# A fused top-k attention and ELU feed-forward kernel: ten steps instead of six in the step-by-step order, first scores head by head, and every second output tile in a bank of the first layer

## The chip, the cores and the metric

The kernel runs on one core of a Trainium2 chip. The metric is the device time of one execution in microseconds (us). The core's engines run side by side, each with its own queue of instructions in program order: TensorE (PE in the profile, with PEld for its weight loads), VectorE (DVE), ScalarE (ACT), GpSimd (POOL) and SyncE (SP), which here issues most DMAs.

## The reference

```python
q, k, v : (8, 8, 576, 64)            # batch, heads, tokens, head size, float32
scores = (q @ k^T) / sqrt(64)
kth    = 32nd largest score of each row
scores = where(scores >= kth, scores, -1e9)
attn   = softmax(scores)             # denominator + 1e-9
x      = (attn @ v)                  # to (8*576, 512)
h      = x @ w_in                    # (512, 2048)
g      = where(h > 0, h, exp(min(h, 0)) - 1)
out    = g @ w_out                   # (2048, 512) -> (4608, 512)
```

The two weight matrices arrive as float64, so the kernel reads them as pairs of 32-bit words and makes float32 of them itself.

## The kernel before, in words

**Attention steps.** The work is cut into 144 steps. A step (class `Step`) is 128 queries of one pair of heads, with all 576 keys: a score tile `sc` of 128 x 2 x 576. Four steps make a token tile of 128 queries over all eight heads (a remainder tile of 64 queries takes two steps), 36 token tiles' worth in all. For one step the engines do this:

- TensorE multiplies queries and keys (`scores`, into PSUM tiles `scps`); ScalarE copies the result to `sc` (L368).
- VectorE finds the 32 largest values of a row in four rounds of eight: `first_max` (MAX8, L373), then three calls of `next_max` (MATCH_REPLACE8, L379, and MAX8, L387). It is 14 passes over 128 x 576 values.
- GpSimd pushes all smaller scores far down. In the later order this is `mask`, three GpSimd passes a head (L399 to L401). In the order of the first steps it is `mask_early`: a small VectorE instruction (`field`, L413), small GpSimd ones (`minus`, `nth`, `pos`, `neg`), a ScalarE Relu (L428) and one GpSimd subtraction (L431).
- ScalarE takes the exponential with its row sums (`exp`, L439; at the end of a token tile it also adds the small constant to the sums, L445); TensorE transposes the result (`trans`, L481, L499) and multiplies by v (`attend`, L532, into `avps`).
- At the end of a token tile `sums` makes reciprocals of the row sums (VectorE, L451 and L452), sends them through DRAM to all partitions (SP, L456 and L468), ScalarE copies `avps` to `xT` (L542), and `normalise` multiplies them on GpSimd (L547).

**Feed-forward pieces.** Token tiles are grouped in 20 blocks of one to three tiles (the first seven blocks hold one tile each). When a block's tiles are normalised, `ffn_pieces` puts its work into a list: `hidden` pieces (first layer, L567, PSUM pool `ps_h` of two banks, tag "h"; then Exp, Relu, Relu on ScalarE, L581 to L583, and a subtraction on GpSimd, L584), then `project` pieces (second layer, L591, PSUM pool `ps_o` of one bank, tag "o"), eight pieces to a token tile; after the eighth ScalarE copies the bank to `osb` (L600) and SP writes it out. Each piece has a price in the code: 0.5 for a hidden piece of a one-tile block, 1.75 for a projection piece. `feed(n, part)` is called twice in a step; it spreads what is in the list over the steps to the next due time (`dues`), at most 6.6 a step in the first half of the run, and takes only pieces whose weights have been decoded.

**Weights.** There are 32 weight pieces. `split_weight` (ScalarE, L182 and L183) and, two slots later, `join_weight` (VectorE L188 and L189, GpSimd L193) decode one. `decode(n, place)` decides at which places of a step a slot is taken: four a step, five in steps 4 and 5. Slots end in step 7.

**The order of the work** is written out by hand in the loop over `n` at the end. For `n < EARLY` it is the early order, step by step: in step `n` the scores of step `n + 2` are computed, and step `n - 1` gets its `exp`, `trans`, `attend` and, if it ends a token tile, `sums` and `normalise`, all inside step `n`. `sums(last)` then stands inside the second `next_max` of the step. After that comes the order by pairs: in an even step the scores of steps `n + 2` and `n + 3`, and `attend` of steps `n - 4` and `n - 3`, so that a token tile is normalised two steps later than in the early order. `turns` says in which steps the queries and keys of a later pair of heads are transposed (L299, L307); `keep_kq` writes them to DRAM and `load_kq` brings them back for later token tiles (five buffers); `load_next` issues the next q and k loads on SP. `warm(n)` issues transposes of the identity on TensorE that nobody reads.

Of the kernel before, what the change touches and what calls it, by code (L numbers as in the profile page):

```python
# [10 lines left out]
FP32 = mybir.dt.float32  # L11
# [50 lines left out]
def kernel(  # L62
# [268 lines left out]
    def scores(u, half, copy=nc.scalar.copy):  # L331
# [35 lines left out]
                product(i, u.hps[0], i, slice(0, P), 0, ks)  # L367
        copy(u.sc[:, :, ks], ps[:, :, 0:HS])  # L368

    def first_max(u):  # L370
        u.m1 = small.tile([P, 2, 8], FP32, tag="m1", name="m1", bufs=2)
        for i in range(2):
            nc.vector.max(u.m1[:, i, :], u.sc[:, i, :])  # L373
        u.wk = wkpool.tile([P, 2, S], FP32, tag="wk", name="wk")
        u.m, u.cur = u.m1, u.sc
# [178 lines left out]
    def ffn_pieces(blk):  # L554
        N = blk.n * P


        G = {1: 4, 2: 2, 3: 1}[blk.n]

        def hidden(f, part):  # L560
            if part == 0 and f % NG == 0:
                blk.gT.append(gpool.tile([P, NG, T], FP32, tag="g", name="gT"))
            if part == 0 and f % G == 0:
                blk.h = ps_h.tile([P, WN], FP32, tag="h", name="hps")
            ps = blk.h[:, 0 : G * N].rearrange("p (f n) -> p f n", f=G)
            for i in range(part * NC // 2, (part + 1) * NC // 2):
                nc.tensor.matmul(  # L567
                    ps[:, f % G, :],
                    w_in[:, i, f * P : (f + 1) * P],
                    blk.xT[:, i, 0:N],  # L570
                    start=(i == 0),
                    stop=(i == NC - 1),
                )
            if part == 0 or f % G < G - 1:
                return

            f0 = (f - G + 1) % NG
            g = blk.gT[f // NG][:, f0 : f0 + G, 0:N]
            n = fpool.tile([P, WN], FP32, tag="n", name="n", bufs=2)
            n = n[:, 0 : G * N].rearrange("p (f n) -> p f n", f=G)  # L580
            nc.scalar.activation(n, ps, AF.Exp)  # L581
            nc.scalar.activation(g, ps, AF.Relu)
            nc.scalar.activation(n, n, AF.Relu, scale=-1.0, bias=1.0)  # L583
            nc.gpsimd.tensor_tensor(g, g, n, ALU.subtract)  # L584

        def project(s, part):
            if part == 0:
                blk.o = ps_o.tile([P, dm], FP32, tag="o", name="ops")
            step = NF // 8
            for f in range(part * step, (part + 1) * step):  # L590
                nc.tensor.matmul(  # L591
                    blk.o[:],
                    blk.gT[f // NG][:, f % NG, s * P : (s + 1) * P],
                    w_out[:, f, :],
                    start=(f == 0),
                    stop=(f == NF - 1),
                )
            if part == 7:
                o = fpool.tile([P, dm], FP32, tag="osb", name="osb", bufs=1)
                nc.scalar.copy(o[:], blk.o[:])  # L600
                for g in blk.tiles[s]:
                    p0 = g.cols.start - s * P
                    nc.sync.dma_start(out[g.rows, :], o[p0 : p0 + g.ql, :])

        t = max(0.25, 0.667 * blk.n / 3)
        return [
            (
                NC / 2 * t,
                lambda f=f, part=part: hidden(f, part),
                max(f // 4 * NC + NC - 1, 17 if f < NG else 19),  # L610
                blk,
            )
            for f in range(NF)
            for part in range(2)
        ] + [
            (1.75, lambda s=s, part=part: project(s, part), NF + (part + 1) * NF // 8 - 1, blk)
            for s in range(blk.n)
            for part in range(8)
        ]

    ffn = []
    owed = [0.0]

    def feed(n, part):
# [18 lines left out]
            owed[0] -= t  # L643


    EARLY = 6
    sizes = {0: (1, 1, 1, 1, 1, 1, 1, 2), 2: (2, 2, 2, 3), B - 2: (2, 2, 2, 2, 1)}
    steps, first, order = [], {}, []
    for b in range(B):
# [37 lines left out]

    def decode(n, place):

        if place in ((2, 3, 4, 5, 6) if n in (4, 5) else (3, 4, 5, 6)):  # L690
            weight_slot()

    todo, turns, blocks_at, behind = {}, {}, {}, {}
# [20 lines left out]
        elif p >= 2:  # L714
            at(p - 1, keep_kq, *pair)

    for u in steps[EARLY + 2 : EARLY + 4]:
        at(EARLY - 1, load_kq, u)
    for hp in range(1, NHP):
        at(hp, load_v, 0, hp)  # L720
    for b in range(1, B):
# [9 lines left out]
    with tc.manual_schedule():  # L731
        load_qk(0, 0)
        nc.scalar.activation(rec[:], rec[:], AF.Copy)
        for hp in (1, 2):
            load_qk(0, hp)
        load_weights(3)
        warm(16)
        for hp in range(2):
            transpose_qk(0, hp, shared=hp == 0)
            steps[hp].kq = {hp: kqT[0, hp]}  # L740
            scores(steps[hp], 0)
            scores(steps[hp], 1, nc.vector.tensor_copy if hp == 0 else nc.scalar.copy)
            if hp == 0:
                load_qk(0, 3)
        load_weights()
        load_v(0, 0)
        first_max(steps[0])
# [4 lines left out]
        for n in range(NS + 4):  # L752
            early = n < EARLY
            now, last, done = (
                steps[n + d] if 0 <= n + d < NS else None for d in (0, -1, -2)
            )
            for fn, args in todo.pop(n, []):
                fn(*args)
            gone = None
            if early:  # L760
                if n + 2 < NHP:
                    transpose_qk(0, n + 2)
                ahead = steps[n + 2]
                ahead.kq = {hp: kqT[0, hp] for hp in ahead.hps}
                for half in range(2):
                    scores(ahead, half)
                if n < EARLY - 1:
                    warm(24)
            elif n % 2 == 0:

                for d in (2, 3):
                    if n + d < NS:
                        for half in range(2):
                            scores(steps[n + d], half)
                    if d == 2:
                        for u in steps[n - 4 : n - 2]:
                            if not u.attended:
                                attend(u)
                                gone = u
                for u in steps[n + 4 : n + 6]:  # L780
                    load_kq(u)
                for fn, args in behind.pop(n, []):
                    fn(*args)
            if n in turns and not early:
                transpose_qk(*turns[n])
                load_next()
            if now and n > 0:
                first_max(now)
            if last and n > EARLY:
                biases(last, early)  # L790
                mask(last, 0)
            if early:
                decode(n, 0)
                feed(n, 0.5)
                if last:
                    exp(last, 0)
                    exp(last, 1)
                next_max(now, (n, 1))
                decode(n, 2)
                if last:  # L800
                    trans(last)
                feed(n, 0.5)
                next_max(now, (n, 3), last)
                decode(n, 4)
                if last:
                    attend(last)
                if n in turns:
                    transpose_qk(*turns[n])
                if n < EARLY - 1:
                    warm(24)  # L810
                next_max(now, (n, 5))
                tile_ends = last and last.ends
                mask_early(now, (lambda: normalise(last.g)) if tile_ends else None)
                decode(n, 6)
                if n >= NHP - 2:
                    load_next()
                continue
            decode(n, 0)
            feed(n, (0.3, 0.7)[n % 2])
            if now:  # L820
                next_max(now, (n, 1))
            decode(n, 2)
            if last:
                if n > EARLY:
                    mask(last, 1)
                exp(last, 0)
            if done and done.n in by_blocks:
                trans_blocks(done)
            elif done and not done.turned:
                trans(done)  # L830
            if now:
                next_max(now, (n, 3))
            decode(n, 4)
            if gone and gone.ends:
                normalise(gone.g)
            feed(n, (0.3, 0.7)[n % 2])
            if now:
                next_max(now, (n, 5))
            decode(n, 6)
            if last:  # L840
                exp(last, 1)
            if done and done.ends and not done.summed:
                sums(done)
            if n in blocks_at:
                transpose_blocks(*blocks_at[n])
# [35 lines left out]
```

## Time and profile before

| | |
|---|---|
| median of 3 runs | 1623.85 us (1623.75 to 1624.57) |
| profiled execution, its own time | 1623.01 us |
| its span in the trace | 1621.2 us |
| PE busy | 1560.3 us (96%) |
| DVE busy | 1474.9 us (91%) |
| POOL busy | 1141.6 us (70%) |
| ACT busy | 905.5 us (56%) |
| mean granted TensorE clock | 0.991 |

The profiled execution's own time is 1.8 us longer than its span. Busy times overlap, so they do not add up to the span. "Idle before" is the time in which an engine had nothing running before an instruction, and the releaser is the instruction whose end let it go on. For TensorE the profile counts two instructions for one float32 product in the code (a `trans` or `transpose_qk` transpose counts once).

### The profile page before, as it was taken

What the parts mean: (1) busy time and instruction counts of PE and PEld (TensorE: products, weight loads), DVE (VectorE), ACT (ScalarE), POOL (GpSimd) and SP (SyncE); (2) the same over time, 40 slices, a digit from 0 to 9 for tenths busy, and PEclk for the clock granted to TensorE, in tenths of its full rate; (3) what the DMA queues carried; (4) which work ended last, traced back from release to release, by engine and by line L of the source; (5) the groups of instructions that cost most, each with busy time, mean ns of one, the idle gap of its engine ahead of it and who ended that gap; (6) DMA issues with size and microseconds to landing.
All of it is one profiled execution on the core that took longest, in us unless ns stands there. A gap on an engine that the chain in (4) does not pass through costs nothing.

```text
span 1621.2 us, 28833 instructions
## 1 busy us (share of the span) xinstructions
PE 1560.3 (96%) x9948; PEld 1066.8 (66%) x9948; DVE 1474.9 (91%) x3070; ACT 905.5 (56%) x1857; POOL 1141.6 (70%) x1448
## 2 busy tenths in 40 slices
PE   7878999999999999999999999999999999999999
PEld 5765778777675858676565665565565585757665
DVE  7999999999999999999999999989999999899700
ACT  6875666555564756565574575465475364545321
POOL 3777777777786878778687687678677676767621
PEclk8989999999999999999999999999999999999999
DMA  9773454442121413232423524333332552453300
GB/s 311 246 219 120 147 180 141 131 129 104 42 111 51 152 58 117 72 94 82 119 71 104 183 80 116 108 102 103 109 113 76 151 161 96 121 135 89 87 13 14
DMA packets 226706, 188.70 MB, mean 116 GB/s; under 512 B 180480, under 2 KB 188672, under 8 KB 226560
## 3 DMA queue, kind: packets, MB, share of 16 engines
q1 hardware_dynamic: 224192, 186.26, 38.1%
q8 instruction: 79, 1.29, 0.3%
q10 hardware_dynamic: 2368, 0.59, 0.2%
q14 instruction: 67, 0.55, 0.1%
HBM read 151.26 MB, written 35.54 MB: 115 GB/s over the span
## 4 chain that ended last, share of the span: by engine, by line
PE 80%; DVE 8%; POOL 5%; ACT 3%; issue 2%; DMA 1%; SPq 0%; DVEq 0%; POOLq 0%; ACTq 0%
PE ops L591 27%; PE hps L567 27%; PE avps L532 9%; PE scps L348 9%; PE eps L481 6%; DVE m L387 3%; DVE wk L379 3%; POOL sc L401 1%; POOL gT L584 1%; POOL wk L399 1%; POOL wk L400 1%; PE eps L499 1%; DVE raw L189 1%; PE qkps L299 0%; DVE m L373 0%
## 5 line engine op out<-in xcount | busy, mean ns | idle before, releaser
L387 DVE MAX8 m<-wk 128x8 f32<-128x576 f32 x864 | 609.8, 748 | 0.0
L567 PE MATMUL hps<-xT,w_in 128*128 128x256 f32 (+2 forms) x2560 | 531.8, 363 | 13.5 <-POOL xT L547 9.1
L591 PE MATMUL ops<-w_out,gT 128*128 128x512 f32 x1152 | 518.8, 596 | 7.5 <-ACT osb L600 7.5
L567 PEld LDWEIGHTS hps<-xT,w_in 128*128 128x128 f32 x2560 | 406.5, 193 | 118.8 <-issue 19.7
L379 DVE MATCH_REPLACE8 wk<-m,wk 128x576 f32<-128x576 f32 x576 | 423.6, 743 | 0.0
L401 POOL TENSOR_TENSOR sc<-sc,wk 128x576 f32<-128x576 f32 x276 | 389.4, 1411 | 23.1
L591 PEld LDWEIGHTS ops<-w_out,gT 128*128 128x128 f32 x1152 | 210.1, 190 | 244.4 <-issue 219.1
L439 ACT ACTIVATE sc<-sc,neg 128x576 f32<-128x576 f32 x288 | 224.1, 779 | 215.0 <-POOL sc L401 210.6
L584 POOL TENSOR_TENSOR gT<-gT,n 128x512 f32<-128x512 f32 (+1 forms) x160 | 186.4, 1169 | 178.7 <-ACT n L583 175.9
L368 ACT COPY sc<-scps 128x576 f32<-128x576 f32 x287 | 169.3, 641 | 118.3 <-PE scps L348 115.4
L399 POOL TENSOR_SCALAR wk<-sc,nth 128x576 f32<-128x576 f32 x276 | 207.1, 750 | 26.9
L379 DVE MATCH_REPLACE8 wk<-m,sc 128x576 f32<-128x576 f32 x288 | 211.8, 744 | 0.0
L373 DVE MAX8 m<-sc 128x8 f32<-128x576 f32 x288 | 201.0, 740 | 0.1
L348 PE MATMUL scps<-kq 64*128 64x288 f32 (+3 forms) x1344 | 181.5, 419 | 20.2 <-ACT sc L368 10.9
L400 POOL TENSOR_SCALAR wk<-wk 128x576 f32<-128x576 f32 x276 | 184.3, 668 | 22.9
L532 PE MATMUL avps<-et,vE 128*64 128x128 f32 (+1 forms) x3200 | 176.7, 266 | 6.0 <-ACT et L486 3.6
L532 PEld LDWEIGHTS avps<-et,vE 128*64 128x64 f32 x3200 | 158.9, 137 | 31.9 <-issue 23.7
L486 ACT COPY et<-eps 128x1024 f32<-128x1024 f32 x132 | 132.7, 1005 | 68.9 <-PE eps L481 67.6
L581 ACT ACTIVATE n<-hps 128x512 f32<-128x512 f32 (+1 forms) x160 | 88.9, 556 | 134.8 <-PE hps L567 132.0
L348 PEld LDWEIGHTS scps<-kq 64*128 64x128 f32 (+1 forms) x1344 | 101.9, 175 | 88.7 <-issue 32.6
L481 PEld LDWEIGHTS eps<-ident,sc 128*128 128x128 f32 x1056 | 122.1, 141 | 49.2 <-issue 31.9
L481 PE MATMUL eps<-ident,sc 128*128 128x128 f32 x1056 | 138.1, 273 | 6.4 <-ACT sc L439 3.4
(74 smaller groups left out, 957.4 us busy)
## 6 DMA issues: line engine op xcount, KB each, us to landing
kq<-kqd SPq DMA_DIRECT2D x152, 576.0 KB
kqd<-kq SPq DMA_DIRECT2D x32, 576.0 KB
rb<-recd SPq DMA_DIRECT2D x64, 128.0 KB
out_dram<-osb SPq DMA_DIRECT2D x32, 256.0 KB
ed<-sc SPq DMA_DIRECT2D x12, 576.0 KB
et<-ed SPq DMA_DIRECT2D x48, 144.0 KB
kin<-in_k_dram SPq DMA_DIRECT2D x18, 256.0 KB
qin<-in_q_dram SPq DMA_DIRECT2D x17, 256.0 KB
```

The costliest lines, as they stand in the source:

```text
L348: nc.tensor.matmul(ps[rows, j, at : at + keys.stop - keys.start], u.kq[hp][r, 1, q0 : q0 + g.ql], u.kq[hp][r, 0, keys], start=True, stop=True,
L373: nc.vector.max(u.m1[:, i, :], u.sc[:, i, :])
L379: nc.vector.match_replace(u.wk[:, i, :], u.m[:, i, :], u.cur[:, i, :], TAKEN)
L387: nc.vector.max(u.m[:, i, :], u.cur[:, i, :])
L399: nc.gpsimd.tensor_scalar(pen, s, u.nth[:, i : i + 1], 2.0**100, ALU.add, ALU.mult)
L401: nc.gpsimd.tensor_tensor(s, s, pen, ALU.add)
L439: nc.scalar.activation(s, s, AF.Exp, bias=u.neg[:, i : i + 1], scale=scale, accum_out=g.den[:, at : at + 1],)
L481: nc.tensor.transpose(ps[:, i, c * P : (c + 1) * P], e[:, k0 + c * P : k0 + (c + 1) * P], ident[:],)
L532: nc.tensor.matmul(g.av[r, hp, 0:ql], vE[g.b, hp][:, i, (c + i) % (J + 1), :], u.et[:, at, q0 : q0 + ql], start=(c == 0), stop=(c == J),)
L567: nc.tensor.matmul(ps[:, f % G, :], w_in[:, i, f * P : (f + 1) * P], blk.xT[:, i, 0:N], start=(i == 0), stop=(i == NC - 1),)
L584: nc.gpsimd.tensor_tensor(g, g, n, ALU.subtract)
L591: nc.tensor.matmul(blk.o[:], blk.gT[f // NG][:, f % NG, s * P : (s + 1) * P], w_out[:, f, :], start=(f == 0), stop=(f == NF - 1),)
```

## The change

1. `EARLY` is 10 instead of 6. Steps 6 to 9 run in the early order. The `warm(24)` calls stay in steps 0 to 4, the transposed score tiles `et` of the first ten steps all go to the same spare buffer, and the keys and queries of steps 10 to 13 are loaded in steps 7 and 8 (before: at the start of steps 6 and 8).
2. `scores_by_head` computes the scores of step 0 head by head: each head's two halves of the keys, then one ScalarE copy of that head. Before, each half of the keys was computed for both heads, and the second copy was VectorE's. Nine idle transposes are put ahead of it.
3. The first weight load is issued before the loads of the third pair of heads, not after them.
4. `project` takes its PSUM bank from `ps_h` for every second token tile.
5. In steps 4 and 5 the fifth weight slot is at place 0 instead of place 2.

```diff
+    def scores_by_head(u):
+
+        u.sc = scpool.tile([P, 2, S], FP32, tag="sc", name="sc")
+        hp = u.hps[0]
+        for i in range(2):
+            ps = ps_x.tile([P, 2, JP], FP32, tag="x", name="scps")
+            r = slice(i * D, (i + 1) * D)
+            for half in range(2):
+                nc.tensor.matmul(
+                    ps[:, half, 0:HS],
+                    u.kq[hp][r, 1, u.g.qt * P : u.g.qt * P + u.g.ql],
+                    u.kq[hp][r, 0, half * HS : (half + 1) * HS],
+                    start=True,
+                    stop=True,
+                )
+            nc.scalar.copy(
+                u.sc[:, i, :].rearrange("p (n k) -> p n k", n=2), ps[:, :, 0:HS]
+            )
...
         def project(s, part):
             if part == 0:
-                blk.o = ps_o.tile([P, dm], FP32, tag="o", name="ops")
+
+                blk.o = (
+                    ps_h.tile([P, WN], FP32, tag="h", name="ops")
+                    if next(tile_count) % 2
+                    else ps_o.tile([P, dm], FP32, tag="o", name="ops")
+                )
...
+    tile_count = iter(range(B * S // P))
...
-    EARLY = 6
+    EARLY = 10
...
-        if place in ((2, 3, 4, 5, 6) if n in (4, 5) else (3, 4, 5, 6)):
+        if place in ((0, 3, 4, 5, 6) if n in (4, 5) else (3, 4, 5, 6)):
             weight_slot()
...
-    for u in steps[EARLY + 2 : EARLY + 4]:
-        at(EARLY - 1, load_kq, u)
+    for u, n in zip(steps[8 : EARLY + 4], (5, 5, 7, 7, 8, 8)):
+        at(n, load_kq, u)
...
         load_qk(0, 0)
         nc.scalar.activation(rec[:], rec[:], AF.Copy)
-        for hp in (1, 2):
-            load_qk(0, hp)
-        load_weights(3)
+        load_qk(0, 1)
+        load_weights(1)
+        load_qk(0, 2)
+        load_weights(2)
         warm(16)
         for hp in range(2):
             transpose_qk(0, hp, shared=hp == 0)
             steps[hp].kq = {hp: kqT[0, hp]}
-            scores(steps[hp], 0)
-            scores(steps[hp], 1, nc.vector.tensor_copy if hp == 0 else nc.scalar.copy)
             if hp == 0:
+                warm(9)
+                scores_by_head(steps[0])
                 load_qk(0, 3)
+            else:
+                for half in range(2):
+                    scores(steps[hp], half)
...
-                ahead.kq = {hp: kqT[0, hp] for hp in ahead.hps}
+                if ahead.n < 8:
+                    ahead.kq = {hp: kqT[0, hp] for hp in ahead.hps}
...
-                if n < EARLY - 1:
+                if n < 5:
                     warm(24)
...
-                if n >= NHP - 2:
+                if n == NHP - 2 or n in turns:
                     load_next()
```

More of the change, by code (lines that the diff above doesn't have):

```diff
@@ L808 @@
                     transpose_qk(*turns[n])
-                if n < EARLY - 1:
+                if n < 5:
                     warm(24)
```

## The prediction

> **What bounds the kernel now.** First the page's busy times and then the table of busy time by stage.
>
> ```profile
> PE 1560.3 (96%) x9948; PEld 1066.8 (66%) x9948; DVE 1474.9 (91%) x3070; ACT 905.5 (56%) x1857; POOL 1141.6 (70%) x1448
> ```
>
> ```profile
> 80.00:100.00 20.00, 14.54 (x125) 12.17 (x125) 19.97 (x36) 16.00 (x29) 14.65 (x16) 1.00 0.61 185
> 100.00:120.00 20.00, 14.65 (x105) 13.38 (x106) 19.96 (x40) 15.34 (x28) 14.68 (x19) 0.74 0.77 236
> 120.00:140.00 20.00, 16.59 (x92) 9.54 (x91) 20.00 (x39) 11.81 (x24) 16.77 (x19) 1.00 0.41 128
> 140.00:160.00 20.00, 16.07 (x107) 10.76 (x106) 19.97 (x43) 10.02 (x20) 13.76 (x18) 0.95 0.35 111
> 160.00:200.00 40.00, 39.87 (x331) 31.15 (x330) 36.79 (x80) 23.74 (x48) 30.07 (x39) 0.98 0.48 150
> 200.00:400.00 200.00, 199.75 (x1619) 151.99 (x1618) 195.08 (x413) 120.70 (x244) 148.46 (x190) 1.00 0.44 135
> 400.00:800.00 400.00, 391.54 (x2532) 274.83 (x2531) 396.88 (x838) 229.16 (x470) 306.42 (x393) 1.00 0.28 90
> 800.00:1200.00 400.00, 393.92 (x2265) 238.65 (x2264) 382.92 (x801) 229.21 (x499) 293.37 (x382) 1.00 0.38 111
> ```
>
> After the stage come its length, then PE, PEld, DVE, ACT, POOL, the clock, the DMA share and GB/s. Three regimes follow each other. To 160 us VectorE is full and TensorE is not: of 80 us it is idle 18. From 160 to 400 TensorE is full and VectorE waits 8 us. From 400 to 800 VectorE is full (99.2%), later TensorE (98.5%) more than VectorE (95.7%). TensorE's work can't shrink much, so a gain is TensorE time that is filled before 160 us, or a wait removed where it is full.
>
> The timeline of TensorE shows what it waits for in the early stage and at an output bank near the end; VectorE's shows the first wait of the second regime.
>
> ```profile
> 105.35 2.29 PE L348 MATMUL scps<-kq 64*128 64x288 f32 x8 [7.53 <-ACT sc L368]
> ...
> 158.02 7.25 PE L567 MATMUL hps<-xT,w_in 128*128 128x128 f32 x48 [2.84 <-POOL xT L547]
> ...
> 1575.38 14.00 PE L591 MATMUL ops<-w_out,gT 128*128 128x512 f32 x32 [0.68 <-ACT osb L600]
> ```
>
> ```profile
> 182.61 0.09 DVE L379 MATCH_VALUE_LOAD wk<-m,sc 128x8 f32 x1 [3.18 <-POOL sc L401]
> ```
>
> At 105 us step 6, the first in pairs, wants two steps' scores; the second stands behind a ScalarE copy that is itself queued behind the Relu of step 5. At 158 us the second token tile reaches the first layer: steps 4 to 7 were done, but the order by pairs normalises them only in step 10.
>
> **The longer early order (steps 6 to 9).** I followed `feed` through its own prices (near real times: a one-tile block's hidden pieces cost 16 and took 14.45 us, its projection 14 and 13.9). The second tile is now normalised in step 8 instead of 10, its due time is 9 instead of 10. Fed up to the end of step 13: before 53.0, after 58.25. The difference is three projection pieces of four, x 1.74 us = 5.2 us of TensorE work done ahead. By step 38, another due time, both stand at 210; so the 5.2 us come out of steps 14 to 37, where TensorE is full, and nothing of it is left for the tail.
>
> Does it fit? TensorE's rows: scores of a step 1.2, `trans` 1.14, `attend` 1.2, a turn 1.3. Step 8 has 7 of feed and 4.8 of these (11.8), step 9 has 10.6, against VectorE's 9.64 (a step without joins); so TensorE falls some 3 us behind there. Steps 10 to 13 need 23 to 25.75 of feed, 4.8 scores, three `trans`, one `attend`, two turns: 37, against 39.9 before and VectorE's 38.6 in four steps. TensorE enters step 14 about where it did, at 190 instead of 190.5, with 5.2 us less to do: **-5.7** at step 38.
>
> VectorE must follow. It loses or gains this:
> - `field` in four steps: the next instruction starts 0.08 later each, +0.3.
> - In steps 6 and 7 GpSimd has 2.8 us of subtraction a step for 5.7 of masks. VectorE's L189 takes 0.68, but 1.78 to 1.88 beside a GpSimd pass (114.59, 124.91): one of these goes at best a step, -0.7 (0 to -2.2).
> - The moved slot: L189 at place 2 of steps 4 and 5 took 1.78 and 1.79, beside a GpSimd join that had been queued behind the subtractions. At place 0 it comes 2.7 us after `field`, when the first subtraction has just begun (2.5), so it can be held there as well: -0.5 (0 to -2.2).
> - `sums` of the second tile moves into step 8. The sums come from ScalarE; step 4 shows the path:
>
> ```profile
> 66.66 0.17 DVE L413 TENSOR_SCALAR field<-m 128x2 uint32<-128x2 uint32 x1
> ...
> 76.29 0.19 DVE L451 RECIPROCAL rec<-den 128x8 f32<-128x8 f32 x1
> ```
>
> ```profile
> 68.24 1.63 ACT L428 ACTIVATE wk<-sc,pos,nth 128x576 f32<-128x576 f32 x2 [1.60 <-POOL pos L420]
> ...
> 73.64 0.21 ACT L445 ACTIVATE den<-den 128x8 f32<-128x8 f32 x1
> ```
>
> The sums are ready 7.2 us after `field`; 1.15 of that was a weight split, which step 8 lacks, so 6 to 7.2. VectorE in step 4 came 9.6 after `field`, with three joins between; in step 8 there are none and it comes after 0.1 + 1.33 + 1.31 + 1.33 + 1.31 = 5.4. It will wait, with MAX8 and all of step 8 queued behind: +1 (0.6 to 1.8; with a hidden group of ScalarE ahead 1.7 more).
> - Waits for `sc` L401: 3.18 in step 13 and 5.7 more in steps 14 to 38. They come from GpSimd queued behind first-layer pieces that TensorE had not finished. With one `attend` less ahead of these in step 12, I take 2 of the 3.18, and leave the 5.7 to give way as TensorE's load falls.
> VectorE's limit at step 38: 0.3 - 0.7 - 0.5 + 1 - 2 - 5.7 - 1 (start, below) = -8.6. TensorE's -5.7 is the smaller gain and decides.
>
> GpSimd in step 8 waits for the reciprocals' way through DRAM (7.5 us from 149.2 to 156.7): about 1.5 us with step 8's subtractions behind it, then `exp` and `trans` of step 8 on TensorE. That is the 3 us lag above. ScalarE gets a Relu pair of 1.63 a step, 6.5 in all, at 12 to 16 us of 20; hidden by its idle time, else it delays the score copies, needed two steps later. SP: the loads for steps 10 and 11 start a step later, behind `load_next`, which waits for a turn's transposes; the scores of step 10 are multiplied in step 8 and read in step 10, so a late load costs TensorE at most, 0 to 3. The q and k loads of the turns stay one to a turn, at the end of the step. The moved slot also puts a split (1.2) ahead of `exp` in steps 4 and 5: hidden by ScalarE's idle 1.9 to 2.7 before each Relu. `et` in one buffer: it is read before the next copy in TensorE's own order, 0.
>
> **The start.** The first MAX8 began at 11.15, after eight products (2.29), ScalarE's copy and VectorE's own copy. By head it needs four products and one copy of 0.64: 7.94 + 1.15 + 0.64 = 9.7, at full clock 9.2. The second head's copy ends 0.64 later, when MAX8 of the first (0.66) does: no wait.
>
> ```profile
> 6.00:8.00 2.00, 0.86 (x9) 0.99 1.37 226
> 8.00:10.00 2.00, 2.00 (x8) 0.50 1.37 201
> ```
>
> The clock fell to 0.50 after 1.1 us without products, and eight products took 2.29 instead of 1.24; nine transposes fill that gap: 0.11 each at full clock (24 took 2.60 at 24.04) or 0.21 (the first 16 took 3.32), from 6.8 to 7.8 or 8.7, so they delay the scores by 0 to 0.8. The Trainium skill, "TensorE: Matmul & The Clock Gate", Part 1, says that the clock halves only after a whole idle window of about 3.4 us, free-running, which this row contradicts unless the slow start counts as idle; by the rule the nine may change nothing, by the row they give 0.5 us, and the sum needs neither.
>
> But VectorE's next wait is for a split at 22.13 (0.69), behind the third pair's copies on ScalarE. That pair's loads now queue behind 1.5 MB of weights (5 us at 300 GB/s), the weights come earlier. From +1.5 to -1.9; I take -1, inside VectorE's limit.
>
> **The output bank.** The waits table has it:
>
> ```profile
> PE ops L591 <- ACT osb L600: 7.5, 11, 0.7
> ...
> PE hps L567 <- ACT gT L582: 4.4, 4, 1.6
> ```
>
> Eleven times TensorE waits 0.7 us for the copy of the tile before. With two banks in turn all go. 1.4 us lie where VectorE is the bound (400 to 800), 6.1 where TensorE is. Against it, `project` now can wait for a bank that the last but one hidden group has just filled; the second line says how often that distance already made TensorE wait, 4 times at 1.1 among some 280 groups. 18 tiles use such a bank: up to 1.4 us. **-4.7** (-7.5 to 0).
>
> **Sum.** 1623.0 (the profiled execution) - 5.7 - 4.7 = 1612.6; the median of before is 0.8 above that execution: 1613.
>
> **Rivals.**
> - *VectorE gets chained in steps 6 to 9* (slower). In each early step the Relu, the exponential and the transposes follow VectorE's last MAX8 through three engines in order. If VectorE must wait for what comes back, as TensorE did for 7.5 us in step 6, four waits of 4 us cost 16: 1623.8 + 16 - 4.7 (banks) - 1 (start) = 1634. It decides against the change from 10.4 / 4 = 2.6 us a step. For it: the early Relu already keeps ScalarE waiting 2.69 us at 102.04 with score copies queued behind. Against: from 40 to 100 us, in the same order and with more ScalarE work, VectorE was busy 59.87 of 60.
> - *Nothing comes of it*. VectorE keeps its pace to step 14, its waits for masks stay, and those for output banks return as waits for hidden groups: 1623.8 - 1 (start) - 1.4 (banks) + 1 (`den`) = 1622.4. For it: the planner evens out at step 38, and VectorE is full before 160 us.
> - *More*. VectorE's terms all at their good ends, 0.3 - 2.2 - 2.2 + 0.6 - 3.2 - 5.7 - 1.9 = -14.3, with TensorE following, and the banks' 7.5: 1602.
>
> **How the numbers follow.** Forecast 0.62 (1607 to 1619), more 0.10, nothing 0.13, chained 0.15. A measurement here can tell about 0.2% from no change. Faster 0.72, same 0.13, slower 0.15. The range 1604 to 1624 leaves out the chained case and a little at the lower end.
>
> **What would show it.** Right: TensorE's waits of 7.5 and 2.8 us gone, a first-layer piece of the second tile near 145 us, a VectorE wait of about 1 us for `den` in step 8, no wait on `osb`, step 38's first MAX8 (431.2 before) some 6 us earlier. Wrong: VectorE below 99% between 100 and 150 us, or TensorE idle as long as before up to 160 us, or new waits of `ops` on L582.

## The result

The changed kernel takes 1630.97 us (median of 6 runs, 1628.56 to 1632.9), the kernel before 1624.21 us (6 runs, 1623.75 to 1625.4). The ratio is 1.0039 with a 95% interval of 1.0026 to 1.0051: slower by about 6.3 us, where 10.8 us less was forecast, in a range from 1604 to 1624. The change is a sum of a gain and a larger loss. Run alone, the output banks are worth -10.4 us and the longer early order costs +14.8 us; the start cannot be told from nothing, and neither can the moved slot, which was run only together with the banks and the start.

### The profile page after: what moved, and what is told of

It reads as the page before. It is cut to its first block, busy times and chain, and to the rows that moved or that the text cites. A ratio compares the mean times of both kernels' runs of the same rounds, so it can differ in the third digit from the quotient of the medians.

```text
span 1627.2 us, 28888 instructions
## 1 busy us (share of the span) xinstructions
PE 1564.3 (96%) x9957; PEld 1072.5 (66%) x9957; DVE 1475.8 (91%) x3073; ACT 911.8 (56%) x1866; POOL 1133.0 (70%) x1444
## 4 chain that ended last, share of the span: by engine, by line
PE 66%; DVE 16%; POOL 6%; ACT 3%; DMA 3%; issue 3%; SPq 2%; DVEq 0%; POOLq 0%; ACTq 0%
PE hps L586 24%; PE ops L615 21%; PE avps L551 7%; PE scps L348 7%; DVE m L406 7%; DVE wk L398 7%; PE eps L500 5%; POOL sc L420 2%; POOL gT L603 1%; DVE m L392 1%; POOL wk L418 1%; POOL wk L419 1%; DMA vE<-in_v_dram 1%; PE qkps L299 1%; DMA ed<-sc 1%
## 5 line engine op out<-in xcount | busy, mean ns | idle before, releaser
L420 POOL TENSOR_TENSOR sc<-sc,wk 128x576 f32<-128x576 f32 x268 | 377.7, 1409 | 22.3
L458 ACT ACTIVATE sc<-sc,neg 128x576 f32<-128x576 f32 x288 | 223.9, 778 | 221.3 <-POOL sc L420 220.4
L418 POOL TENSOR_SCALAR wk<-sc,nth 128x576 f32<-128x576 f32 x268 | 199.6, 745 | 26.2
L419 POOL TENSOR_SCALAR wk<-wk 128x576 f32<-128x576 f32 x268 | 178.7, 667 | 22.1
L348 PE MATMUL scps<-kq 64*128 64x288 f32 (+1 forms) x1336 | 179.9, 418 | 11.8 <-ACT kq L294 6.7
L600 ACT ACTIVATE n<-hps 128x512 f32<-128x512 f32 (+1 forms) x160 | 88.7, 555 | 132.8 <-PE hps L586 127.9
```

The costliest lines, as they stand in the source:

```text
L348: nc.tensor.matmul(ps[rows, j, at : at + keys.stop - keys.start], u.kq[hp][r, 1, q0 : q0 + g.ql], u.kq[hp][r, 0, keys], start=True, stop=True,
L418: nc.gpsimd.tensor_scalar(pen, s, u.nth[:, i : i + 1], 2.0**100, ALU.add, ALU.mult)
L420: nc.gpsimd.tensor_tensor(s, s, pen, ALU.add)
L458: nc.scalar.activation(s, s, AF.Exp, bias=u.neg[:, i : i + 1], scale=scale, accum_out=g.den[:, at : at + 1],)
```

## The profile after

The profiled execution took 1628.94 us, with a span of 1627.2 us. The page's busy times:

```profile
PE 1564.3 (96%) x9957; PEld 1072.5 (66%) x9957; DVE 1475.8 (91%) x3073; ACT 911.8 (56%) x1866; POOL 1133.0 (70%) x1444
```

They hardly differ from before. The table by stage (stage, length, PE, PEld, DVE, ACT, POOL, clock, DMA share, GB/s) shows where the order went wrong:

```profile
100.00:120.00 20.00, 12.47 (x101) 11.28 (x99) 16.71 (x31) 12.81 (x25) 13.39 (x14) 0.83 0.39 112
120.00:140.00 20.00, 11.33 (x57) 7.01 (x58) 19.50 (x40) 11.40 (x22) 12.38 (x18) 0.74 0.23 81
140.00:160.00 20.00, 17.62 (x95) 10.42 (x94) 17.04 (x38) 11.31 (x23) 7.98 (x15) 1.00 0.61 190
160.00:200.00 40.00, 38.19 (x266) 28.92 (x265) 34.23 (x73) 24.84 (x48) 25.66 (x32) 0.96 0.57 170
200.00:400.00 200.00, 199.23 (x1631) 150.91 (x1630) 196.22 (x415) 122.21 (x249) 149.11 (x193) 1.00 0.43 134
```

TensorE was to be fuller between 100 and 200 us, by the 5.2 us of projections done ahead. It is emptier: 12.47 + 11.33 + 17.62 + 38.19 = 79.6 us, against 87.2 before (14.65 + 16.59 + 16.07 + 39.87). VectorE, which was full to 160 us, loses 3.3 us from 100 to 120 and 3.0 from 140 to 160.

TensorE's timeline shows the holes, with the releaser in brackets:

```profile
98.31 3.39 PE L586 MATMUL hps<-xT,w_in 128*128 128x128 f32 x28
108.33 1.97 PE L500 MATMUL eps<-ident,sc 128*128 128x128 f32 x8 [6.63 <-ACT sc L458]
...
127.83 1.97 PE L500 MATMUL eps<-ident,sc 128*128 128x128 f32 x8 [8.74 <-ACT sc L458]
...
142.66 1.04 PE L500 MATMUL eps<-ident,sc 128*128 128x128 f32 x8
...
158.28 2.40 PE L586 MATMUL hps<-xT,w_in 128*128 128x128 f32 x20
```

The waits of 7.53 and 2.84 us that the prediction wanted to remove are gone. In their place stand 6.63 us in step 6 and 8.74 us in step 7, ahead of the transposes of `trans(last)`. The eight transposes after each hole take 1.97 us, where they take 1.04 in step 8, at 142.66, in a stage with the clock at 1.00. The second token tile reaches the first layer at 158.28 us; before it was 158.02, and the forecast was near 145.

ScalarE's timeline shows why the transposes are so late, and VectorE's what that does to it:

```profile
102.22 1.62 ACT L447 ACTIVATE wk<-sc,pos,nth 128x576 f32<-128x576 f32 x2 [2.18 <-POOL pos L439]
103.75 0.65 ACT L182 ACTIVATE w_out<-w_out 128x512 f32<-128x512 f32 x1
104.31 0.65 ACT L183 ACTIVATE w_out<-w_out 128x512 uint32<-128x512 uint32 x1
104.86 1.15 ACT L368 COPY sc<-scps 128x576 f32<-128x576 f32 x2
105.91 0.60 ACT L600 ACTIVATE n<-hps 128x512 f32<-128x512 f32 x1
...
107.40 0.79 ACT L458 ACTIVATE sc<-sc,neg 128x576 f32<-128x576 f32 x1
...
112.95 0.60 ACT L600 ACTIVATE n<-hps 128x512 f32<-128x512 f32 x1 [1.44 <-PE hps L586]
...
114.44 0.68 ACT L182 ACTIVATE w_out<-raw 128x512 f32<-128x512 f32 x1
```

```profile
100.64 0.17 DVE L432 TENSOR_SCALAR field<-m 128x2 uint32<-128x2 uint32 x1
...
115.15 1.05 DVE L188 TENSOR_SCALAR w_out<-w_out 128x512 uint32<-128x512 uint32 x1 [3.21 <-ACT w_out L182]
...
142.86 0.20 DVE L470 RECIPROCAL rec<-den 128x8 f32<-128x8 f32 x1 [3.33 <-ACT den L464]
...
182.75 0.09 DVE L398 MATCH_VALUE_LOAD wk<-m,sc 128x8 f32 x1 [4.72 <-POOL sc L420]
```

The exponential of step 5 (L458, 107.40) stands on ScalarE behind the Relu, a weight split, two score copies and a hidden group (the Exp, Relu, Relu that follow a first-layer tile), while TensorE idles. Restarted at 108.33, TensorE delivers its next hidden group late, ScalarE's L600 waits 1.44 us for that, and behind it stands the weight split (L182, 114.44) that VectorE needs: VectorE waits 3.21 us. The same lag comes back in step 8 at `den` (3.33) and in step 12 at a mask (4.72; before, 3.18 in step 13).

The start of each step is the first MAX8 of it on VectorE. Against before, the changed kernel is 0.2 us late at step 6, 4.9 at step 7, 8.4 at step 9, 10.9 at step 14, 9.3 at step 38, 15.9 at step 90 and 7.8 at step 143. The prediction had 6 us early at step 38. (In the thirteen profiles with the old start, step 6 begins between 101.48 and 103.52 us, the kernel before being the earliest, so up to 2 us of such a difference can be the execution's.)

At the output banks the profile has no idle time left:

```profile
L615 PE MATMUL ops<-w_out,gT 128*128 128x512 f32 x1152 | 516.3, 597 | 0.0
```

## The experiments

Times are medians; the ratio is to runs of the kernel before on the same chip, with its 95% interval. For the parts alone the difference from before is taken from the ratio, later from the medians. "Profiled" spans have a run's noise in them: the same kernel's runs spread over up to 6 us.

### The parts alone

**Banks alone** (before, with the choice of `blk.o` from the change):

```diff
-                blk.o = ps_o.tile([P, dm], FP32, tag="o", name="ops")
+                blk.o = (
+                    ps_h.tile([P, WN], FP32, tag="h", name="ops")
+                    if next(tile_count) % 2
+                    else ps_o.tile([P, dm], FP32, tag="o", name="ops")
+                )
...
+    tile_count = iter(range(B * S // P))
```

> The kernel before with the bank alternation alone (part 4). If the longer early order is the whole loss, this is 3 to 6 us faster than before, with no wait of ops on osb (before: 7.5 us in 11 times). Rival: the banks tie the second layer to the first, the waits come back on gT and the time is the same within 1 us or some us slower.

1613.17 us, ratio 0.9936 (0.9924 to 0.9948): -10.4 us. The output layer's group before, then the same group with the banks and the one wait that was feared:

```profile
L591 PE MATMUL ops<-w_out,gT 128*128 128x512 f32 x1152 | 518.8, 596 | 7.5 <-ACT osb L600 7.5
...
L595 PE MATMUL ops<-w_out,gT 128*128 128x512 f32 x1152 | 515.9, 595 | 0.0
...
PE hps L567 <- ACT gT L582: 4.3, 4, 1.6
```

All eleven waits (7.5 us) went and no new ones came: 4.3 us on L582, as before (4.4). The profiled spans differ by 7.3 (1613.9 against 1621.2), which is the waits. Some of the gain lies between 400 and 800 us, the stage where the prediction had said that a TensorE wait costs nothing: VectorE is idle 1.7 us there instead of 3.1. The medians' further 3 us are not in this profile: its execution was the slowest of five (1615.72), the output layer's own time fell by 2.9 us and the first layer's grew by 4.0. The other pairs of kernels that differ in the banks alone agree that the banks are worth 8 to 11 us (below).

**The start alone** (scores by head, nine transposes, weights' loads):

```diff
-        for hp in (1, 2):
-            load_qk(0, hp)
-        load_weights(3)
+        load_qk(0, 1)
+        load_weights(1)
+        load_qk(0, 2)
+        load_weights(2)
...
+                warm(9)
+                scores_by_head(steps[0])
...
```

> The kernel before with the new start alone (parts 2 and 3: scores by head, nine idle transposes, weights loaded earlier). In the profile after, step 0 began 1.03 us earlier and step 1 only 0.24. Both theories: within 1 us of before. Rival for the loss: if the earlier weights push something else back, 2 us or more slower.

1624.36 us, ratio 1.0001 (0.9993 to 1.001): nothing.

**The early order alone**, with the loads and `load_next` that belong to it:

```diff
-    EARLY = 6
+    EARLY = 10
...
```

> The kernel before with EARLY = 10 alone (part 1 with what it needs: the loads of steps 10 to 13, the calls of load_next). Theory of the early order: step 14 begins about 11 us later than before (202.2 in the profile after against 191.3), VectorE waits about 3 us for a weight split in step 6 and 3 us for the sums in step 8, and the time is 8 to 14 us over before. Rival (the loss comes from the banks or from the moved slot): step 14 within 3 us of before and the time within 3 us.

1638.85 us, ratio 1.0091 (1.0078 to 1.0104): +14.8 us. Its TensorE has the same two holes and its VectorE the same three waits; a fourth comes at 651.56 us:

```profile
108.64 1.97 PE L481 MATMUL eps<-ident,sc 128*128 128x128 f32 x8 [6.97 <-ACT sc L439]
...
128.12 1.97 PE L481 MATMUL eps<-ident,sc 128*128 128x128 f32 x8 [8.75 <-ACT sc L439]
```

```profile
115.43 1.05 DVE L188 TENSOR_SCALAR w_out<-w_out 128x512 uint32<-128x512 uint32 x1 [3.17 <-ACT w_out L182]
...
651.56 0.09 DVE L379 MATCH_VALUE_LOAD wk<-m,sc 128x8 f32 x1 [3.41 <-POOL sc L401]
```

**Everything but the early order** (the change with `EARLY` back at 6, and with it the loads and `load_next`):

```diff
-    EARLY = 10
+    EARLY = 6
...
```

> The kernel after with EARLY back at 6 (parts 2 to 5 stay). Theory of the early order: no wait of VectorE in steps 6 and 8, step 14 within 1.5 us of 191.3, and 3 to 7 us faster than before. Rival: still slower than before by 2 us or more.

1613.98 us, ratio 0.9937 (0.9926 to 0.9949): start and slot add nothing to the banks. The parts sum to -10.4 + 14.8 + 0.2 = +4.6 against +6.3 (4.2 to 8.3) for the whole.

### Why the early order is slow far behind it

It is 9.6 us late at step 38 but 16.0 at step 84, although nothing of it lies there. `feed` carries a remainder, `owed`, from step to step. At the start of step 39 the list of pieces is the same in both kernels, but the remainder is -0.714 before and 0.047 with the longer early order. So later steps take other numbers of pieces: 20 steps from 40 to 74, and steps 117 and 118, get one more or one fewer.

**The early order with the old remainder** (the diff), and **the kernel before with the new one** (the same edit with 0.04687499999997202):

```diff
         for n in range(NS + 4):
+            if n == 39:
+                owed[0] = -0.7141666666666979
             early = n < EARLY
```

> e3_early10 (the longer early order alone) with the planner's carry (owed) at the start of step 39 set to the value that it has before the change, -0.714 instead of 0.047; from there on the pieces are the same, step for step, as before. Theory (the shifted pieces cost what is lost after step 38): step 38 begins 9 to 10 us late as in e3_early10 (9.6), step 143 no more than 11 late (15.3 in e3_early10), the time 4 to 6 us under e3_early10. Rival (a late start by itself makes more waits): step 143 still 14 to 16 us late.

> The kernel before with the planner's carry at step 39 set to the value of e3_early10 (0.047 instead of -0.714), and nothing else. Theory: nothing changes to step 38, and then 4 to 6 us are lost: 1628 to 1630. Rival: within 1.5 us of before.

1634.52 us (1.0065, 1.005 to 1.008), 4.3 less than without, and 1628.83 us (1.0029, 1.0018 to 1.004), 4.4 more than before. One remainder, exchanged both ways, is worth the same amount. It is lost on VectorE between 400 and 800 us: with the new remainder VectorE is idle 7.1 us there instead of 3.1 in the kernel before, and 6.4 instead of 2.5 with the early order. VectorE's timeline of the kernel before with the new remainder has the wait that the early order had at 651.56, while with the old remainder VectorE has no wait between 640 and 670 us:

```profile
643.56 0.09 DVE L379 MATCH_VALUE_LOAD wk<-m,sc 128x8 f32 x1 [3.41 <-POOL sc L401]
```

and its table row for that stage (stage, length, DVE, clock, DMA share, GB/s) is

```profile
400.00:800.00 400.00, 392.86 (x830) 1.00 0.27 88
```

The next experiments all keep the old remainder, so that only the steps up to 38 are in question: +10.5 us are left.

### Which wait in steps 6 to 13

**A weight slot of step 6 earlier**, so that VectorE's split is ahead of the late hidden group:

```diff
-        if place in ((2, 3, 4, 5, 6) if n in (4, 5) else (3, 4, 5, 6)):
+        places = (2, 3, 4, 5, 6) if n in (4, 5) else (3, 4, 5, 6)
+        if place in ((0, 4, 5, 6) if n == 6 else places):
```

> e5_carry with the first weight slot of step 6 at place 0 instead of 3, so that its split is ahead of the hidden pieces' activations on ScalarE. Theory (VectorE's 3.2 us in step 6 come from a split queued behind activations that wait for TensorE): no wait for w_out L182 in step 6, step 7 begins at most 2 us late (5.2 in e3_early10), and the time is 2 to 4 us under e5_carry. Rival (the wait only moves, because ScalarE and TensorE are late anyway): step 9 as late as before (8.6).

**The turns of steps 7 to 9 later**, so that a turn's copy is not ahead of the Relu and the exponentials that `den` needs:

```diff
-                if n in turns:
+                if n in turns and n < 6:
                     transpose_qk(*turns[n])
...
                 mask_early(now, (lambda: normalise(last.g)) if tile_ends else None)
+                if n in turns and n >= 6:
+                    transpose_qk(*turns[n])
```

> e5_carry with the turn's transposes of steps 7 to 9 behind mask_early instead of ahead of it. Theory (the sums of step 8 are late because the Relu of step 7 stands behind the copy of that turn on ScalarE): the Relu of step 7 no longer waits for TensorE, the wait for den in step 8 falls from 3.3 us to under 1.5, step 9 is about 2 us less late than in e3_early10 (8.6), and the time is 1 to 3 us under e5_carry. Rival: the wait for den stays over 2.5 us.

1633.70 us (1.0058, 1.0043 to 1.0073) and 1635.69 us (1.007, 1.0053 to 1.0087): -0.8 and +1.2, both within the error, where 2 to 4 and 1 to 3 us less were expected. VectorE's waits in the first (before the edit 3.08, 3.26 and 4.71):

```profile
118.35 1.04 DVE L188 TENSOR_SCALAR w_out<-w_out 128x512 uint32<-128x512 uint32 x1 [1.20 <-ACT w_out L182]
...
145.01 0.20 DVE L451 RECIPROCAL rec<-den 128x8 f32<-128x8 f32 x1 [4.36 <-ACT den L445]
```

and in the second:

```profile
143.25 0.20 DVE L451 RECIPROCAL rec<-den 128x8 f32<-128x8 f32 x1 [2.10 <-ACT den L445]
...
185.43 0.09 DVE L379 MATCH_VALUE_LOAD wk<-m,sc 128x8 f32 x1 [5.80 <-POOL sc L401]
```

Each edit shortened the wait that it aimed at, and the next wait grew by 1.1 us. So these waits look like symptoms of one lag.

**The step's whole feed ahead of the transposes** in steps 6 to 9, so that TensorE has work while the exponential is on its way:

```diff
-                feed(n, 0.5)
+                feed(n, 1.0 if n > 5 else 0.5)
...
-                feed(n, 0.5)
+                feed(n, 0.0 if n > 5 else 0.5)
```

> e5_carry with the whole feed of steps 6 to 9 ahead of the transposes of the step before, instead of half of it. Theory (in the early order TensorE stands still until the exponential of the step that VectorE has just finished, 6.6 and 8.8 us in steps 6 and 7, because only half a step's feed lies ahead of it): these two waits fall by 5 us or more together, the turn of step 7 is copied earlier, the wait for den in step 8 falls under 2 us, step 14 begins 7 to 9 us late instead of 12, the time 2 to 5 us under e5_carry (1634.5). Rival (the path from VectorE's last MAX8 over GpSimd and ScalarE sets the step, whatever TensorE does): step 14 within 1 us of e5_carry's.

1626.98 us, ratio 1.0018 (1.0008 to 1.0027): 7.5 us less than without it. TensorE's timeline:

```profile
107.77 1.16 PE L567 MATMUL hps<-xT,w_in 128*128 128x128 f32 x8 [3.21 <-ACT gT L582]
110.53 1.97 PE L481 MATMUL eps<-ident,sc 128*128 128x128 f32 x8 [1.60 <-ACT sc L439]
...
124.75 1.41 PE L481 MATMUL eps<-ident,sc 128*128 128x128 f32 x8 [0.87 <-ACT sc L439]
```

and VectorE's:

```profile
137.08 0.20 DVE L451 RECIPROCAL rec<-den 128x8 f32<-128x8 f32 x1 [0.67 <-ACT den L445]
...
177.16 0.09 DVE L379 MATCH_VALUE_LOAD wk<-m,sc 128x8 f32 x1 [4.74 <-POOL sc L401]
```

The hole of step 7 is down to 0.87 us, that of step 6 to 3.21 and 1.60, VectorE's 3.1 us wait of step 6 is gone and that for `den` is 0.67. So 7.5 of the 10.5 us come from TensorE having no work ahead of the transposes.

**All three edits together**:

> e5_carry with the three repairs together: feed ahead, the first slot of step 6 at place 0, the turns behind mask_early. Theory: no wait over 1.5 us on VectorE in steps 6 to 9, step 10 begins 1 to 4 us late instead of 9, the time 5 to 8 us under e5_carry: 1627 to 1630, still not under before, since the wait of step 12 for a mask stays. Rival (each repair moves the wait to the next engine): step 10 still over 6 us late.

1635.11 us, ratio 1.006 (1.0045 to 1.0075), where 1627 to 1630 was expected. The other two edits took back all that the feed had gained. TensorE's timeline:

```profile
110.74 2.08 PE L567 MATMUL hps<-xT,w_in 128*128 128x128 f32 x8 [6.05 <-ACT gT L582]
...
135.89 2.29 PE L348 MATMUL scps<-kq 64*128 64x288 f32 x8 [3.56 <-ACT kq L294]
```

With the fed pieces ahead TensorE depends on ScalarE's hidden group, and the earlier split now stands in front of that: it waits 1.75 us for GpSimd's join and puts the group (L581) off from 106.64 to 109.63; TensorE waits 6.05 us instead of 3.21. The later turn puts its copy (134.85) behind the Relu of step 7 (133.32), and step 10's scores wait 3.56 us for it. Edits that each moved about 1 us alone cost 8 us on top of the feed.

**No feed in step 10** (at both of its calls of `feed`), on top of the feed ahead, against the 4.74 us wait of step 12:

```diff
-            feed(n, (0.3, 0.7)[n % 2])
+            feed(n, 0.0 if n == 10 else (0.3, 0.7)[n % 2])
```

> e8_feed_first with no feed-forward pieces in step 10 (they follow in steps 11 to 38; from step 39 the pieces are those of before). Theory (the mask of step 10 waits on GpSimd behind a first-layer group that TensorE, 7 us behind VectorE at the change of order, delivers late): the wait of 4.7 us in step 12 falls under 2, step 14 begins 2 to 3 us late instead of 5, the time 1624 to 1626 (e8: 1627.0). Rival (the group then stands ahead of another mask, in step 11 or 12): the sum of VectorE's waits in steps 11 to 14 stays over 4 us and the time within 1 us of e8.

1627.01 us, ratio 1.0017 (1.0008 to 1.0026): nothing. VectorE's timeline:

```profile
174.09 0.09 DVE L379 MATCH_VALUE_LOAD wk<-m,sc 128x8 f32 x1 [1.18 <-POOL sc L401]
...
226.25 0.09 DVE L379 MATCH_VALUE_LOAD wk<-m,sc 128x8 f32 x1 [2.70 <-POOL sc L401]
```

The wait shrank by 3.6 us and 2.7 of it came back in a later step. At step 14 this kernel is only 1.9 us late, at step 18 again 4.7 and at step 38 6.0 (the feed ahead alone: 5.4).

The holes can also be read from TensorE's windows alone (stage, length, PE, clock, DMA share, GB/s), first the early order alone, then with the feed ahead (and the old remainder):

```profile
100.00:200.00 100.00, 79.25 (x514) 0.90 0.47 143
```

```profile
100.00:200.00 100.00, 86.19 (x568) 0.93 0.49 147
```

Before it was 87.2. Even the best early order, without its holes, leaves TensorE no fuller than the order by pairs.

### The banks with repaired early orders

The banks were added to the last three kernels: to all three edits, to the feed ahead, and to the feed ahead with no feed in step 10.

> e9_three with the bank alternation. If the parts add up, the time of e9_three less 10 (e1_banks took 10.4 off before). If the repaired early order is worth keeping it comes under 1613, the time of the banks alone; I expect 1616 to 1620.

> e8_feed_first with the bank alternation. If the parts add up: 1627.0 less 10.4, about 1616.6, over the banks alone (1613.2).

> e11_no_feed10 with the bank alternation: e11's time less 10.4, so 1614 to 1616 by the first theory, still no better than the banks alone (1613.2); by the rival about 1616.6.

1625.55 us (1.0005, 0.9995 to 1.0014), 1616.36 us (0.9952, 0.9937 to 0.9968) and 1618.62 us (0.9961, 0.9946 to 0.9976): 9.6, 10.6 and 8.4 us below the same kernels without the banks. None is better than the banks alone, 1613.17, the lowest time of this study; everything but the early order, 1613.98, cannot be told from it.

## Why the prediction was wrong

- **"Does it fit?" is the step that failed.** It summed TensorE's work per step and VectorE's time per step and set the larger against the other. It did so for steps 8 and 9 and for 10 to 13; steps 6 and 7, where the holes came, were not summed at all. But TensorE takes its work in order: in the early order only a step's scores and half a step's feed lie ahead of `trans(last)`, and that needs the exponential of a step which VectorE has only just finished. Nothing was summed for the way from VectorE's last MAX8 over GpSimd, ScalarE's Relu, splits, copies and hidden group to the exponential: `field` ends at 100.81 and the transposes start at 108.33, 7.5 us later. In the order by pairs the transposes of a step come a step later, behind more of other steps' work. Putting the feed into that time gave 7.5 of the 14.8 us back.
- **The -5.7 us at step 38 never came.** TensorE between 100 and 200 us was busy 79.6 us instead of 87.2, and with the holes repaired 86.2. The waits of 7.53 and 2.84 were removed as forecast, but in the repaired kernel TensorE is still idle 14.1 us between 100 and 240 us, against 13.1 before: for copies of transposed scores, hidden activations, exponentials and turn copies instead of mostly score copies.
- **"Nothing of it is left for the tail" was wrong by 4.3 us.** The list was the same at the end of step 38, as the prediction said; the planner's remainder was not, by 0.76 of a unit. The prediction followed `feed` through its prices and read off the pieces, not the remainder.
- **The wait for `den` in step 8** was forecast at +1 (0.6 to 1.8) and came to 3.33. The path was right and the size wrong: it took ScalarE to be on time, and the lag of steps 6 and 7 stood ahead of it. Without that lag it was 0.67, inside the forecast.
- **The L401 wait** was to lose 2 of 3.18 us; it became 4.72, a step earlier. Taking 3.6 us of it away changed nothing, so its size in the sum meant nothing either.
- **The start** was forecast at -1, out of a range from +1.5 to -1.9 that was not followed further. The first MAX8 came 1.03 us earlier than in the profile before, but by step 1 only 0.24 of that was left, and the start alone gave 0.2 us more, which is nothing. Much of the 1.03 belongs to that one profile: in the twelve others with the old start the first MAX8 begins at 10.18 to 11.03 us, with the new start at 10.12 to 10.64.
- **The clock.** The row on which the nine transposes rest was one execution's. The twelve other profiles with the old start have the same gap of 1.1 us ahead of the first scores, and in all of them the clock is 1.00 from 8 to 10 us and the eight products take 1.24 us, as in the banks alone:

```profile
8.49 1.24 PE L348 MATMUL scps<-kq 64*128 64x288 f32 x8 [1.14 <-DVE kq L292]
```

With the nine transposes the clock is 1.00 too, and the products take 1.37: as a rule there was nothing for them to win. The Trainium skill, "TensorE: Matmul & The Clock Gate", Part 1, makes the drop depend on a whole idle window of about 3.4 us. In the sixteen traces the granted clock does change only in steps of 3.41 us, which fall at another moment in each execution, but the stretch ahead of a drop is not always idle: in 110 drops TensorE was busy for 0 to 55% of it. The kernel before had the 55%, ahead of the drop at 7.96 us (stage, length, PE, clock, DMA share, GB/s):

```profile
4.54:7.96 3.42, 1.88 (x17) 1.00 1.30 214
7.96:11.37 3.41, 3.41 (x14) 0.50 1.29 235
```

So the slow start was a matter of where the step fell in that execution. The holes of 6.6 and 8.7 us are long enough to meet a step wherever it falls, and there the clock dropped 3.2 and 2.8 us after TensorE had stopped.

- **The output bank** was right in its mechanism and mis-sized: -4.7 against -10.4. The 1.4 us that "lie where VectorE is the bound" were gained too, and the 1.4 set aside for new waits on L582 did not occur. With these two put back the term is the 7.5 us of the waits table; the profiled spans show 7.3 of it.
- **The rival "VectorE gets chained"** is nearest to what happened: it had 1634 us and a chance of 0.15, and 1631.0 was measured. That the time fits so well is partly luck: its 16 us for the chain stand for some 10.5 us of chain and 4.3 of remainder, and its banks were worth 5.7 too little. Its mechanism was right in two of the four steps, with waits of 3.21 and 3.33 us, above its threshold of 2.6. The argument that spoke against it, VectorE full from 40 to 100 us in the same order, had little force: the first piece of the first layer ran at 86.0 us, so in most of that stretch no hidden group stood in ScalarE's queue.

**What stays open.** The early order with feed ahead and the old remainder is still 2.5 us slower than before. From 100 us on its TensorE is as busy as before (1484.3 and 1484.6 us) and idle 3.5 us more, in small pieces between 100 and 800 us; no single wait carries it, and the one that was tried did not. The 3 us of the banks that the profile does not show are open as well.

## What to carry to other kernels

An earlier or later order of the same work cannot be judged by each engine's sum per step: follow one step's chain through every in-order queue, and ask what each engine has left to do while that chain is under way. A single wait on an engine that lags is often only where the lag shows; an edit that fills the hole ahead of it is worth several that move what stands behind it. A planner that rounds carries an edit's effect far past its steps, so compare its carried state, not only its list; and a wait of the bound engine for a free buffer is worth its whole time when a second buffer is at hand.

## What the runs showed of the hardware

- After 6.63 and 8.74 us without work, TensorE's next eight transposes took 1.97 us instead of 1.04; the granted clock was 0.83 and 0.74 in these 20 us stages.
- VectorE's shift L188 (part of a weight's join) took 1.05 us instead of 0.41 at 115.15, beside GpSimd passes from 114.63 to 117.36, and the two-column `field` 1.06 instead of 0.17 at 119.26, beside one from 119.01 to 120.29. So lag on one engine moved costs onto another that no wait shows.
- The granted clock changed only in steps of 3.41 us in all sixteen traces. Ahead of a drop to 0.50 TensorE had been busy 0 to 55% of such a step, and steps at 1.00 that were not followed by a drop had at least 42%, the last of the program aside. So a gap of 1.1 us at the start halved the clock in one execution and left it at 1.00 in twelve, and eight products took 2.29 and 1.24 us.
